# A seven-product group's four sums in one block on VectorE or all on GpSimd, one more group, and a finer copy of the small projection

## The chip, the cores and the metric

One core of one Trainium2 chip runs the whole program. The metric is the device time of one launch in microseconds (us); lower is better. Everything is written out in one kernel file: the instructions of each engine, their order, and the semaphores between the engines.

## The reference

```python
B, T, D, K, U = 2, 4000, 512, 5, 8
h  = gelu(conv1d(x,  w1, K taps))[:, ::2]        # (2, 2000, 512)
f  = gelu(conv1d(h,  w2, K taps))[:, ::2]        # (2, 1000, 512)
fe = f @ w_f                                     # (2, 1000, 512)
ge = g @ w_g                                     # (2, 8, 512)
j  = tanh(fe[:, :, None, :] + ge[:, None, :, :]) # (2, 1000, 8, 512)
out = j @ w_o                                    # (2, 1000, 8, 512)
```

All inputs and the output are bf16. The two convolutions have five taps, padding 2, and keep every second position. The last product is the largest part: 16,000 rows of j by the 512 x 512 matrix w_o.

## The kernel before, in words

**Stages.** Until about 130 us of the profiled execution, TensorE (PE) is mostly busy with the two convolutions. They are cut into 21 units; the first few products of fe and the product ge lie at the end of this stage. From there to about 246 us is the joint stage: the rest of fe, the tanh, and the product with w_o. The 16,000 rows of j are 125 tiles of 128 rows. The 64 activations that make j (`tanh`) each take one row of ge as their bias and up to 1,000 columns of feT as input, and write bf16 into two ring buffers, `jT` and `jX`, from which PE reads.

**Plain tiles and groups of seven.** A tile can be multiplied in the plain way: `Plain` issues four matmuls of 512 columns into one PSUM bank, and the bank is evicted into `ost` and stored. Or four neighbouring tiles form a group (`Seven`): the 2 x 2 block product is done with seven products instead of eight, as Strassen and Winograd do it. A product is four matmuls of 256 columns (two tiles, two blocks of the inner dimension), so a group has 28 of them. For this it needs four sums of blocks of j (`sums`, line 1094, the buffers `ss`), four sums of blocks of w_o (`wsums`, once, the buffer `tw`), and more work behind the products:

- `p1` multiplies into a bank A, and a copy of the result goes to an SBUF buffer `sn` (`keep`).
- `p5` does the same with a bank D.
- `p2` takes a bank of its own, adds the kept product 1 and writes the result to `og` (`out`, an addition on VectorE).
- `p6` accumulates onto bank A, is kept again, and `p3` accumulates onto D and adds that.
- `p7` and `p4` accumulate onto A in turn; each is followed by its own `out`.

Product 6 therefore waits until product 1 has been kept, product 7 until product 6 has been kept, and product 4 until the output of product 7 has been read from the bank. On PE the products of neighbouring groups are interleaved: 1 of this group, 7 of the last, 5, 2, 6, 4 of the last, 3. Fillers stand between them: plain tiles, pieces of the convolution (`piece`) and products of fe. Of the eight banks, `take()` hands out the one that has been free longest.

**FeSeven.** The first quarter of fe is done in the same seven-product way, with sums on VectorE (`fsums`). Its first product needs fT; its `p1` and `p2` take the next banks of the cycle. The bank of product 2 is the one in which ge was computed.

**ge.** `ge` (line 812 and following) does sixteen small matmuls into one bank, 64 columns in all, which ScalarE copies to `geT`.

**Who does which, and in which order.** `Plan` collects all operations of the program in the order in which the program text makes them. The table `ORDER` then lists, for each engine, the numbers of the operations that it issues, as differences from the one before. Operations that may go to one of two engines (`flex`: the evictions and the sums) go where the table has them. `edges` finds from the buffers which operation must wait for which, `schedule` lays the table out in time, and `emit` writes out the instructions with the semaphore waits. So nothing is decided on the chip: every engine issues its list in order, and each instruction waits until the ones it depends on on other engines are done. SyncE (SP) issues nearly all transfers, also from such a list.

In the kernel before, each of the four sums of a group goes to VectorE (DVE) or GpSimd (POOL) by itself. At the end, `emit` adds waits between the two engines by its own timetable: a sum on POOL that would start within 1.5 us behind the start of a sum on DVE waits for that one:

```python
for o in sorted((o for o in ops if o.port), key=lambda o: (self.start[o.idx], o.eng == "pool")):
    if o.eng == "dve":
        near = o.idx
    elif near is not None and self.start[near] > self.start[o.idx] - 1.5:
        o.after.append(near)
```

**The start.** ScalarE (ACT) begins with fourteen activations of one column (`warm`, the loop over `NPRE`), each reading one element of a two-element buffer and writing the other, and each waiting for the one before. Behind them it copies part of the transposed x (`eo`), which the first convolution matmuls read.

Of the kernel before, what the change touches and what calls it, by code (L numbers as in the profile page):

```python
# [30 lines left out]
        4 2 3""",  # L31
    "act": """
# [9 lines left out]
        3 12 7 1 8 1""",  # L42
    "dve": """
# [9 lines left out]
        7 6 17 67 -61 18 -37 46 35 -29 4 17 36 -10 3 -36 13 16 27 7 -21 27 15 -3 9 8 2""",  # L53
    "pool": """
        1 55 1 -55 1 1 1 28 218 1 -217 258 -252 253 8 89 174 150 1 54 -2 1 -31 33 33 2 -1 38 -36 35 40 -38 37 34 2 33
        -32 33 32 -30 31 1 1 33 1 28 1 1 28 155 -154 1 27 2 -1 33 -31 32 1 28 2 -1 31 -29 30 1 26 37 -36 37 1 1 33 34
        -33 34 -32 33 1 29 2 -1 33 2 -1 33 2 -1 35 2 -1 36 2 -1 28 -26 27 1 27 1 27 1 1""",
    "sp": """
        6 15 1 1 1 1 1 1 1 1 1 1 1 2 2 1 1 1 1 2 1 1 1 1 1 248 1 1 1 1 1 1 2 1 1 1 1 1 254 1 1 145 3 33 33 4 1 1 30 4 33
        4 1 1 33 4 31 4 1 1 29 4 29 4 1 1 29 4 25 4 1 1 25 4 25 4 1 1 27 4 27 4 1 1 25 4 25 4 1 1 19 1 11 4 21 11 4 19  # L60
        11 4 17 11 1 1 4 17 11 1 1 4 17 11 4 1 1 19 11 4 21 1 11 4 25 4 23 1 1 4 23 4 19 1 1 7 3 3 5 5""",
}

# [49 lines left out]
class Op:  # L113
    __slots__ = ("eng", "fn", "reads", "writes", "dma", "signal", "count", "sem", "val", "idx", "cost", "pin", "after", "wire", "alt", "port", "slack")


class Plan:
# [12 lines left out]
    def op(self, eng, fn, reads=(), writes=(), cost=0.1):  # L130
        o = Op()
        o.eng, o.fn, o.dma, o.signal, o.idx, o.alt, o.port = eng, fn, False, False, len(self.ops), None, self.port
        o.reads, o.writes, o.cost, o.pin, o.after = tuple(reads), tuple(writes), cost, self.pin, list(self.hold)
        self.ops.append(o)
        return o
# [7 lines left out]
    def dma(self, eng, fn, reads=(), writes=(), sem=None, nbytes=524288, rate=330e3, slack=0.0):  # L143

        o = Op()
        o.eng, o.fn, o.dma, o.signal, o.idx, o.alt, o.port = eng, fn, True, False, len(self.ops), None, False
        o.reads, o.writes, o.cost, o.pin, o.after, o.wire = tuple(reads), tuple(writes), 0.43, True, [], nbytes / rate
        o.slack = slack
        if sem is None:
            sem = [self.nc.alloc_semaphore(f"s_d{o.idx}"), 0]  # L150
        sem[1] += 16
        o.sem, o.val = sem[0], sem[1]
        self.ops.append(o)
        return o
# [81 lines left out]
    def emit(self, block, tail):  # L236
# [3 lines left out]
        near = None  # L240
        for o in sorted((o for o in ops if o.port), key=lambda o: (self.start[o.idx], o.eng == "pool")):
            if o.eng == "dve":
                near = o.idx
            elif near is not None and self.start[near] > self.start[o.idx] - 1.5:
                o.after.append(near)
# [3 lines left out]
        for o in ops:  # L249
            need = {}  # L250
            for j, w in pred[o.idx].items():
                q = ops[j]
# [64 lines left out]
def bass_standalone__seq2seq_rnn_t_joint__speech_kernel(  # L317
# [38 lines left out]
    NPRE = 14  # L356
    TAPS = (0, 4, 2, 1, 3)
    NX = 2

    with ExitStack() as es:  # L360
# [140 lines left out]
        for _ in range(NPRE):  # L501
            act(warm[0:1], warm[1:2], ACT.Gelu_apprx_tanh)
# [311 lines left out]
        def ge():  # L814
            c0 = bank()
            for m in range(NK):
                mm(ps.cols(c0 + m * BU, BU), [(wg_sb[k, m * P:(m + 1) * P], gT[k]) for k in range(NK)], True, True)
            act(geT[:], ps.cols(c0, NK * BU), ACT.Copy)
# [253 lines left out]
        class Seven:  # L1072
# [15 lines left out]
            def sums(self):  # L1088
                S = self.S
                eng = "dve" if self.n in (0, 1) else "pool"  # L1090
                pl.port = True
                for i, x, y, op in ((0, self.a(1, 0), self.a(1, 1), add), (1, S[0], self.a(0, 0), sub),
                                    (2, self.a(0, 0), self.a(1, 0), sub), (3, self.a(0, 1), S[1], sub)):
                    fn = lambda e, o=S[i], x=x, y=y, op=op: e.tensor_tensor(out=o.ap, in0=x.ap, in1=y.ap, op=op)  # L1094
                    alt = {"pool": (fn, 1.12), "dve": (fn, 0.34)}
                    pl.flex({k: alt[k] for k in (("dve", "pool"))}, (x, y), (S[i],))
                pl.port = False
# [130 lines left out]
        gaps = (1, 3, 5, 7)  # L1228
        jts = [2 + 4 * i for i in range(S1)]
        j = 2 + 4 * S1  # L1230
        for n in range(13):
# [75 lines left out]
```

## Time and profile before

| | before |
|---|---|
| time, median of 3 runs | 250.69 us (250.52 to 250.94) |
| the profiled execution: time / span | 250.55 us / 248.7 us |
| PE matmuls, busy | 243.8 us (98%), 1938 on record |
| PE weight loads (PEld), busy | 182.6 us (73%) |
| DVE, busy | 208.0 us (84%) |
| ACT, busy | 197.6 us (79%) |
| POOL, busy | 100.7 us (41%) |
| sums of groups (L1094), in the joint stage | DVE 26, 17.7 us; POOL 86, 98.3 us |
| granted TensorE clock | 1.0 |

The span is what the profile sees, from the first instruction to the last; the time is what the launch took. PEld is the loading of weights into TensorE, which overlaps its matmuls. In the rows below, a line of the timeline has the start in us from the beginning of the span, the length in us, engine, source line, operation, output and inputs, shapes, and how many instructions in a row it stands for; square brackets hold what the engine waited for just before it, and how long. A row of the view of waits has the waiting instruction, an arrow to what released it, and then the sum of the waits, their count, and the longest. A row of windows has the stretch, its length, and the busy time of each engine.

### The profile page before, as it was taken

The numbers are of one execution on the slowest core, as the hardware profiler recorded it, in microseconds if no ns is written. First come the engines' busy times: TensorE is split into PE (matmuls) and PEld (weight loads), VectorE is DVE, ScalarE is ACT, GpSimd is POOL, SyncE is SP. The second block draws the span as 40 slices with busy tenths as digits, with TensorE's granted clock in tenths as the row PEclk, the third lists the DMA queues.
The fourth block names the chain that finished last, engine by engine and source line by source line (L and its number), as shares of the span: only waits on it lengthen the run. The fifth ranks groups of instructions, "written<-read, shape, count | busy, mean of one in ns | idle before, by whom it ended". The sixth has DMA issues, their size and how long they took to land.

```text
span 248.7 us, 5271 instructions
## 1 busy us (share of the span) xinstructions
PE 243.8 (98%) x1938; PEld 182.6 (73%) x1944; DVE 208.0 (84%) x371; ACT 197.6 (79%) x349; POOL 100.7 (41%) x107
## 2 busy tenths in 40 slices
PE   7999999999999999999999999999999999999994
PEld 3879976666666666666566888777788878777883
DVE  1799996967999994796957889778999999996793
ACT  8787948458786475643699999999999999998672
POOL 1000000000000000000008988978799999999530
PEclk9999999999999999999999999999999999999999
DMA  6999999989000061000001043323345554454547
GB/s 212 319 224 179 126 209 173 193 169 355 31 3 0 0 209 48 0 4 0 0 3 42 31 147 106 100 87 127 109 156 161 172 188 162 160 182 137 192 153 249
DMA packets 54871, 31.83 MB, mean 128 GB/s; under 512 B 31902, under 2 KB 54590, under 8 KB 54846
## 3 DMA queue, kind: packets, MB, share of 16 engines
q1 hardware_dynamic: 54558, 31.34, 47.2%
q8 instruction: 15, 0.25, 0.5%
q10 hardware_dynamic: 288, 0.16, 0.2%
q14 instruction: 10, 0.08, 0.1%
HBM read 7.60 MB, written 16.38 MB: 96 GB/s over the span
## 4 chain that ended last, share of the span: by engine, by line
PE 86%; ACT 7%; DMA 2%; issue 1%; DVE 1%; SPq 0%; DVEq 0%; ACTq 0%
PE acc L461 86%; ACT jT L453 3%; DMA w_sb<-in_w_dram 2%; ACT sn L563 1%; ACT og L563 1%; ACT jX L453 1%; DVE og L448 1%; ACT sd L453 1%; DVE sn L564 0%; DVE og L564 0%; PE acc L599 0%; ACT fT L453 0%; SPq L479 0%; SPq L488 0%; ACT ost L453 0%
## 5 line engine op out<-in xcount | busy, mean ns | idle before, releaser
L448 DVE TENSOR_TENSOR og<-acc,sn 128x512 bf16<-128x512 f32 x84 | 54.7, 682 | 5.1 <-PE acc L461 5.1
L453 ACT ACTIVATE jT<-feT,geT 128x1000 bf16<-128x1000 f32 (+5 forms) x60 | 57.5, 1017 | 0.3 <-DVE feT L448 0.3
L1094 POOL TENSOR_TENSOR ss<-jT 128x512 f16<-128x512 bf16 x34 | 39.7, 1182 | 35.2 <-DVE ss L1094 33.3
L461 PE MATMUL acc<-tw,ss 128*128 128x256 f16 x336 | 46.0, 273 | 0.0
L461 PE MATMUL acc<-row,w_sb 128*128 128x334 bf16 (+2 forms) x224 | 39.2, 297 | 0.0
L461 PEld LDWEIGHTS acc<-tw,ss 128*128 128x128 f16 x336 | 32.3, 98 | 7.5 <-ACT sn L563 0.5
L461 PE MATMUL acc<-wo_sb,jT 128*128 128x256 bf16 (+1 forms) x205 | 33.1, 283 | 0.2
L563 ACT ACTIVATE sn<-acc 128x512 f32<-128x512 f32 x48 | 29.7, 628 | 3.4 <-PE acc L461 2.8
L564 DVE COPY sn<-acc 128x512 f32<-128x512 f32 x36 | 24.6, 685 | 6.3 <-PE acc L461 6.0
L453 ACT ACTIVATE hT<-acc 128x334 bf16<-128x334 f32 (+3 forms) x36 | 15.4, 430 | 17.4 <-PE acc L461 16.9
L461 PEld LDWEIGHTS acc<-row,w_sb 128*128 128x128 bf16 x224 | 21.2, 97 | 9.3 <-DVE acc L605 0.7
L453 ACT ACTIVATE sd<-acc 128x334 f32<-128x334 f32 (+2 forms) x48 | 20.5, 432 | 8.7 <-PE acc L461 7.4
L461 PEld LDWEIGHTS acc<-wo_sb,jT 128*128 128x128 bf16 x208 | 20.2, 98 | 5.1
L1094 POOL TENSOR_TENSOR ss<-ss,jT 128x512 f16<-128x512 f16 x19 | 22.3, 1179 | 2.4 <-DVE ss L1094 1.9
L445 POOL MEMSET hT<- 128x8 bf16 (+2 forms) x6 | 0.8, 148 | 55.5 <-ACT hT L453 43.0
L448 DVE TENSOR_TENSOR row<-row 128x1336 bf16<-128x1336 bf16 (+2 forms) x24 | 19.1, 806 | 0.0
L1094 POOL TENSOR_TENSOR ss<-jT,ss 128x512 f16<-128x512 bf16 x15 | 17.5, 1169 | 2.4 <-DVE ss L1094 2.4
L453 ACT ACTIVATE jX<-feT,geT 128x1000 bf16<-128x1000 f32 (+3 forms) x20 | 18.4, 965 | 0.0
L605 DVE SCALAR_TENSOR_TENSOR acc<-acc,sd 128x334 f32<-128x334 f32 (+2 forms) x24 | 11.7, 488 | 7.6 <-PE acc L461 7.5
L461 PE MATMUL acc<-xp,w_t 128*128 128x334 bf16 (+1 forms) x96 | 17.6, 305 | 0.0
L461 PE MATMUL acc<-hT,w_t 128*128 128x334 bf16 x96 | 17.6, 304 | 0.0
L461 PE MATMUL acc<-wo_sb,ss 128*128 128x256 bf16 x112 | 17.1, 273 | 0.0
(129 smaller groups left out, 473.4 us busy)
## 6 DMA issues: line engine op xcount, KB each, us to landing
out_dram<-og SPq DMA_DIRECT2D x42, 256.0 KB, 2.2
w_sb<-in_w_dram SPq DMA_DIRECT2D x10, 512.0 KB, 5.9
out_dram<-og SPq DMA_DIRECT2D x14, 128.0 KB, 2.3
out_dram<-ost SPq DMA_DIRECT2D x10, 128.0 KB, 1.9
xr<-in_x_dram SPq DMA_DIRECT2D x1, 512.0 KB, 3.2
wf_sb<-in_w_f_dram SPq DMA_DIRECT2D x1, 512.0 KB, 4.2
wg_sb<-in_w_g_dram SPq DMA_DIRECT2D x1, 512.0 KB, 5.2
wo_sb<-in_w_o_dram SPq DMA_DIRECT2D x1, 512.0 KB, 6.8
```

The lines of the kernel that those rows point to most:

```text
L445: pl.op("pool", lambda e: e.memset(v.ap, 0.0), (), (v,))
L448: pl.op(eng, lambda e: e.tensor_tensor(out=o.ap, in0=a.ap, in1=b.ap, op=op), (a, b), (o,), 0.02 + 2.14e-3 * o.ap.free_size() if eng == "po ...
L453: pl.op("act", lambda e: e.activation(o.ap, i.ap, func, scale=scale, bias=0.0 if bias is None else bias.ap), rd, (o,), o.ap.free_size() * ...
L461: ins = e.matmul(o.ap, lhsT=l.ap, rhs=r.ap, start=start and n == 0, stop=stop and n == len(pairs) - 1, skip_group_check=not check)
L563: pl.flex({"act": (lambda e: e.activation(o.ap, v.ap, ACT.Copy), 0.05 + n * 0.833e-3), "dve": (lambda e: e.tensor_copy(out=o.ap, in_=v.ap) ...
L564: "dve": (lambda e: e.tensor_copy(out=o.ap, in_=v.ap), 0.065 + n * 1.04e-3)}, (v,), (o,))
L605: pl.op(eng, lambda e: e.scalar_tensor_tensor(out=o.ap, in0=a.ap, scalar=f, in1=b.ap, op0=ALU.mult, op1=add), (a, b), (o,), vec_cost(o, (a ...
L1094: fn = lambda e, o=S[i], x=x, y=y, op=op: e.tensor_tensor(out=o.ap, in0=x.ap, in1=y.ap, op=op)
```

## The change

1. **Sums.** 29 groups of seven instead of 28, and 9 plain tiles instead of 13: the plain tiles that stand between the last groups go from pairs behind groups 1, 3, 5 and 7 of the later list to pairs behind 1 and 5. For ten of the groups (`ONV`, counted from 0) all four sums are on DVE, in one block with nothing of DVE between them: the first one waits for all the inputs of the four, and each of the others stands right behind the one before. For the other nineteen all four are on POOL. The order within a group is now sum 0, 2, 1, 3. The rule in `emit` is gone; in its place is a table, `AFTER`, with ten pairs: one sum on POOL that waits for the last sum of a block on DVE.
2. **geT.** The copy of the 64 columns of ge from PSUM to `geT` is cut in 24 (`NG`) copies of two or three columns, all on ACT.
3. **warm.** One activation instead of fourteen.
4. **The order.** `ORDER` is written anew for all engines. In the convolutions a few of the evictions and of the scaled copies have changed places between ACT and DVE. In the joint stage, products and fillers stand in a partly different order on PE. The engines' lists differ as follows: PE has 16 matmuls of 512 columns less and 28 of 256 more. DVE has 40 sums instead of 26, three more of the additions that write `og`, three more plain copies to `og`, one copy to `ost` less, and one copy to `sn` less. ACT has four copies to `sn` more, two to `og` less, three to `ost` less, 24 copies to `geT` instead of one, and one `warm` instead of fourteen. POOL has 76 sums instead of 86. Of the 24 copies to `geT`, the first 22 stand before an activation that makes part of fT, and two behind it.

```diff
 ORDER = {
     "pe": """
-        48 1 1 1 1 1 1 1 3 2 2 6 1 -5 1 1 1 4 1 1 1 1 2 2 1 1 1 1 1 1 1 1 1 1 1 1 1 1 1 1 1 1 1 1 1 1 1 68 11 15 -24 1
+        35 1 1 1 1 1 1 1 3 2 2 6 1 -5 1 1 1 4 1 1 1 1 2 2 1 1 1 1 1 1 1 1 1 1 1 1 1 1 1 1 1 1 1 1 1 1 1 68 11 15 -24 1
...
+AFTER = """
+    779:726 780:748 817:854 928:963 1091:1060 1120:1244 1213:1153 1317:1346 1408:1445 1566:1538"""
...
-        near = None
-        for o in sorted((o for o in ops if o.port), key=lambda o: (self.start[o.idx], o.eng == "pool")):
-            if o.eng == "dve":
-                near = o.idx
-            elif near is not None and self.start[near] > self.start[o.idx] - 1.5:
-                o.after.append(near)
+        for word in AFTER.split():
+            i, j = map(int, word.split(":"))
+            ops[i].after.append(j)
...
-    NPRE = 14
+    ONV = (0, 1, 4, 7, 10, 13, 16, 19, 22, 25)
...
+    NG = 24
...
-        for _ in range(NPRE):
-            act(warm[0:1], warm[1:2], ACT.Gelu_apprx_tanh)
+        act(warm[0:1], warm[1:2], ACT.Gelu_apprx_tanh)
...
-            act(geT[:], ps.cols(c0, NK * BU), ACT.Copy)
+            cut = [NK * BU * i // NG for i in range(NG + 1)]
+            for i, j in zip(cut, cut[1:]):
+                act(geT[i:j], ps.cols(c0 + i, j - i), ACT.Copy)
...
-                for i, x, y, op in ((0, self.a(1, 0), self.a(1, 1), add), (1, S[0], self.a(0, 0), sub),
-                                    (2, self.a(0, 0), self.a(1, 0), sub), (3, self.a(0, 1), S[1], sub)):
+                for i, x, y, op in ((0, self.a(1, 0), self.a(1, 1), add), (2, self.a(0, 0), self.a(1, 0), sub),
+                                    (1, S[0], self.a(0, 0), sub), (3, self.a(0, 1), S[1], sub)):
                     fn = lambda e, o=S[i], x=x, y=y, op=op: e.tensor_tensor(out=o.ap, in0=x.ap, in1=y.ap, op=op)
-                    alt = {"pool": (fn, 1.12), "dve": (fn, 0.34)}
-                    pl.flex({k: alt[k] for k in (("dve", "pool"))}, (x, y), (S[i],))
+                    if self.n in ONV:
+                        o = pl.op("dve", fn, (x, y) if i else (x, y, self.a(0, 0), self.a(0, 1)), (S[i],) if i else tuple(S[q] for q in range(4)), 0.34)
+                        o.glue = op is not add
+                        if o.glue:
+                            o.after.append(o.idx - 1)
+                    else:
+                        pl.op("pool", fn, (x, y), (S[i],), 1.12)
...
-        gaps = (1, 3, 5, 7)
+        gaps = (1, 5)
...
-        for n in range(13):
+        for n in range(14):
```

More of the change, by code (lines that the diff above doesn't have):

```diff
@@ L17 @@
     "pe": """
[13 rows of a table removed]
-        4 2 3""",
-    "act": """
[9 rows of a table removed]
-        3 12 7 1 8 1""",
-    "dve": """
[9 rows of a table removed]
-        7 6 17 67 -61 18 -37 46 35 -29 4 17 36 -10 3 -36 13 16 27 7 -21 27 15 -3 9 8 2""",
[13 rows of a table added]
+        3 1 2 1 2 1 2 1 6 1 2 1 7 1 2 1 2 1 -11 1 12 1 2 1 2 1 8 1 -4 1 6 3 3 1 4 2 3""",
+    "act": """
[9 rows of a table added]
+        71 -32 -19 23 27 -37 -55 81 -50 65 -12 18 10 -79 82 8 6 10 13 6 10 11 6 6 15 7 1 8 1""",
+    "dve": """
[9 rows of a table added]
+        3 6 2 8 7 8 3 3 3 63 1 1 1 -42 3 -11 24 19 -26 23 6 -15 40 6 -15 29 7 6 10 6 7 6 10 11 -7 13 6 9 -3 9 8 2""",
     "pool": """
-        1 55 1 -55 1 1 1 28 218 1 -217 258 -252 253 8 89 174 150 1 54 -2 1 -31 33 33 2 -1 38 -36 35 40 -38 37 34 2 33
-        -32 33 32 -30 31 1 1 33 1 28 1 1 28 155 -154 1 27 2 -1 33 -31 32 1 28 2 -1 31 -29 30 1 26 37 -36 37 1 1 33 34
-        -33 34 -32 33 1 29 2 -1 33 2 -1 33 2 -1 35 2 -1 36 2 -1 28 -26 27 1 27 1 27 1 1""",
+        1 42 1 -42 1 1 1 15 218 1 -217 258 -252 253 8 89 174 227 -1 2 35 -34 33 2 1 73 1 1 33 -32 33 1 66 -65 66 1 33
+        -32 33 1 1 57 191 -189 1 -2 28 1 1 1 61 31 -29 -1 2 29 1 64 -63 65 34 -33 34 1 56 -55 56 1 35 -34 33 66 -64 63
+        -62 64 31 -30 31 1 58 -57 58 1 26 -25 53 -29 30 -28 29 -28 29""",
     "sp": """
-        6 15 1 1 1 1 1 1 1 1 1 1 1 2 2 1 1 1 1 2 1 1 1 1 1 248 1 1 1 1 1 1 2 1 1 1 1 1 254 1 1 145 3 33 33 4 1 1 30 4 33
-        4 1 1 33 4 31 4 1 1 29 4 29 4 1 1 29 4 25 4 1 1 25 4 25 4 1 1 27 4 27 4 1 1 25 4 25 4 1 1 19 1 11 4 21 11 4 19
-        11 4 17 11 1 1 4 17 11 1 1 4 17 11 4 1 1 19 11 4 21 1 11 4 25 4 23 1 1 4 23 4 19 1 1 7 3 3 5 5""",
-}
+        6 2 1 1 1 1 1 1 1 1 1 1 1 2 2 1 1 1 1 2 1 1 1 1 1 248 1 1 1 1 1 1 2 1 1 1 1 1 254 1 1 168 3 33 33 4 1 1 30 4 33
+        4 1 1 33 4 31 4 1 1 29 4 29 4 1 1 29 4 25 4 1 1 25 4 25 4 1 1 27 4 27 4 1 1 25 4 25 4 1 1 19 1 11 4 21 11 4 25 4
+        25 1 1 4 19 11 4 1 1 17 11 4 27 1 1 4 27 4 25 1 1 4 25 4 23 1 1 4 23 4 19 1 1 7 3 3 5 5""",
+}
+AFTER = """
+    779:726 780:748 817:854 928:963 1091:1060 1120:1244 1213:1153 1317:1346 1408:1445 1566:1538"""
 class View:
@@ L113 @@
 class Op:
-    __slots__ = ("eng", "fn", "reads", "writes", "dma", "signal", "count", "sem", "val", "idx", "cost", "pin", "after", "wire", "alt", "port", "slack")
+    __slots__ = ("eng", "fn", "reads", "writes", "dma", "signal", "count", "sem", "val", "idx", "cost", "pin", "after", "wire", "alt", "port", "slack", "glue")
 class Plan:
@@ L132, in op @@
         o.eng, o.fn, o.dma, o.signal, o.idx, o.alt, o.port = eng, fn, False, False, len(self.ops), None, self.port
+        o.glue = False
         o.reads, o.writes, o.cost, o.pin, o.after = tuple(reads), tuple(writes), cost, self.pin, list(self.hold)
@@ L146, in dma @@
         o.eng, o.fn, o.dma, o.signal, o.idx, o.alt, o.port = eng, fn, True, False, len(self.ops), None, False
+        o.glue = False
         o.reads, o.writes, o.cost, o.pin, o.after, o.wire = tuple(reads), tuple(writes), 0.43, True, [], nbytes / rate
```

60 rows, old and new, of the table ORDER are left out of this document.

## The prediction

> **What bounds the kernel now.** I read the page first, then the view of waits, then the timeline at each place where TensorE (PE) or its weight loads (PEld) waited.
>
> ```profile
> span 248.7 us, 5271 instructions
> PE 243.8 (98%) x1938; PEld 182.6 (73%) x1944; DVE 208.0 (84%) x371; ACT 197.6 (79%) x349; POOL 100.7 (41%) x107
> ```
> ```profile
> POOL ss L1094 <- DVE ss L1094: 39.3, 10, 32.6
> PEld acc L461 <- ACT eo L453: 0.9, 1, 0.9
> PEld acc L461 <- DVE acc L605: 0.7, 3, 0.2
> PEld acc L461 <- ACT sn L563: 0.5, 2, 0.3
> PEld acc L461 <- DMA w_sb<-in_w_dram: 0.3, 1, 0.3
> ```
> ```profile
> 130.00:246.00 116.00, 115.29 (x952) 92.37 (x956) 101.43 (x167) 109.28 (x169) 98.33 (x86) 1.00 0.43 139
> ```
>
> PE is busy 98% of the span, but a busy PE may still be a waiting one, because ends of matmuls are modelled. So the waits count: after the start (the eo and w_sb rows) PE's loads wait only some tenths of a us in all. The second thing to see is which row is missing: no row has PE or PEld waiting for a sum of POOL (GpSimd) or of DVE. The 39.3 us in the first row are POOL's own waiting for DVE, 32.6 of them before the joint stage began. In that stage (the last row: PE, PEld, DVE, ACT, POOL) all four are nearly full, but only PE's matmuls stand end to end. So the time falls by what is taken from PE's list and from its few gaps, and rises by each wait that becomes longer than what PE has queued in front of it. Faster sums alone are worth nothing.
>
> **Part 1: 29 groups instead of 28.** Four plain tiles (16 matmuls, 512 wide) leave; one group (28 matmuls, 256 wide) comes. What a matmul costs is the distance of the starts, not its modelled duration:
>
> ```profile
> 130.87 0.81 PE L461 MATMUL acc<-wo_sb,jT 128*128 128x512 bf16 x3
> 131.52 0.73 PE L461 MATMUL acc<-row,w_sb 128*128 128x334 bf16 x4
> ...
> 239.34 1.04 PE L461 MATMUL acc<-tw,ss 128*128 128x256 f16 x8
> 240.21 0.60 PE L461 MATMUL acc<-wo_sb,jX 128*128 128x256 bf16 x4
> ```
>
> Three starts of 512 in 131.52 - 130.87 = 0.65 us: 0.217 each. Eight of 256 in 0.87: 0.109 each. So 16 x 0.217 - 28 x 0.109 = 3.47 - 3.05 = **0.42 us less PE work**. With PE end to end, all of it is on the path.
>
> **Part 2: the gaps in the joint stage.** There are two, both a keep of product 1 (sn) that ACT does late, so that product 6, which writes the same bank, waits:
>
> ```profile
> 176.95 1.02 ACT L453 ACTIVATE jX<-feT,geT 128x808 bf16<-128x808 f32 x1
> 177.05 1.04 PE L461 MATMUL acc<-tw,ss 128*128 128x256 f16 x8
> 177.81 1.13 ACT L563 ACTIVATE sn<-acc 128x512 f32<-128x512 f32 x2
> 177.93 0.60 PE L461 MATMUL acc<-wo_sb,jT 128*128 128x256 bf16 x4
> 178.51 0.33 PEld L461 LDWEIGHTS acc<-tw,ss 128*128 128x128 f16 x4 [0.26 <-ACT sn L563]
> ```
> ```profile
> 187.14 1.09 ACT L563 ACTIVATE sn<-acc 128x512 f32<-128x512 f32 x2
> 187.29 0.60 PE L461 MATMUL acc<-wo_sb,jT 128*128 128x256 bf16 x4
> 187.80 0.33 PEld L461 LDWEIGHTS acc<-tw,ss 128*128 128x128 f16 x4 [0.19 <-ACT sn L563]
> ```
>
> Four matmuls from 177.93 end their turn at 178.37; the next start is at 178.51: 0.14 us lost, since ACT was inside a tanh when product 1 ended. From 187.29 likewise 187.73 against 187.80: 0.07. These are groups 9 and 12 (counted from 0). In the new order group 9's keep of product 1 is DVE's, with no tanh ahead of it, and around group 12 ACT has the keeps of products 5 and 1 in a row with no tanh between. Both gaps should go: **0.21 us**. What is late next is the ordinary distance from product 1 to product 6, mostly three products of 0.44 us, in which a keep of 0.6 us fits. The three short waits behind DVE acc (L605) I leave where they are.
>
> **Part 3: sums in blocks.** DVE's sums go from 26 to 40, POOL's from 86 to 76.
>
> ```profile
> L1094 POOL TENSOR_TENSOR ss<-jT 128x512 f16<-128x512 bf16 x34 | 39.7, 1182 | 35.2 <-DVE ss L1094 33.3 <-DVE og L448 0.9 <-PE acc L461 0.9
> L1094 DVE TENSOR_TENSOR ss<-jT,ss 128x512 f16<-128x512 bf16 x8 | 6.9, 863 | 0.0
> L448 DVE TENSOR_TENSOR tw<-wo_sb x2: 420/422/425, 115.7 to 116.0; 128x512 f16<-128x512 bf16 x2
> 237.09 4.87 DVE L448 TENSOR_TENSOR og<-acc,sn 128x512 bf16<-128x512 f32 x8
> ```
> ```profile
> 130.00:246.00 116.00, 17.74 (x26) 98.33 (x86) 1.00 0.43 139
> ```
>
> A sum alone on DVE takes 0.42 us (the weight sums tw, least, middle and most in ns, with POOL idle); beside POOL's sums 0.86. A block without POOL is 4 x 0.42 = 1.7 us; if its first sum meets one of POOL's, up to 1.18 more, 2.9. The Trainium skill, page "SBUF — State Buffer", section "SBUF: two separate sides", calls this an exclusive lock of the shared port pair: whichever engine starts first holds it for its instruction. The rows agree (0.86 against 0.42). By that rule too a block pays at most once, and the sum stays as it is.
>
> DVE: 40 x 0.42 = 16.8 us, with ten full collisions 28.6, against 17.7 for the 26 of before (the last row above, that of the joint stage's sums on DVE and POOL; 0.68 each); also four more evictions (three og additions, three og copies, one ost and one sn less), 0.61 each by the row at 237.09 (4.87 / 8): 2.4. That is +1.5 to +13 us, likelier +4, since a collision rarely meets a POOL sum at its very start. DVE idles 116 - 101.4 = 14.6 us in the stage, so it fits, less easily than before. POOL: ten sums less, 11.8 us; its waits for ten blocks, 17 us, replace some 6.7 (39.3 - 32.6): about as full as before, and nobody waited for it. ACT: three ost and two og less, four sn more: one eviction less. The cost to PE I take as **zero**; the cover is what PE has between a product and the next use of its bank. The first eviction behind most blocks has 2.2 to 2.9 us. If that cover fails the price is the second rival's.
>
> **Part 4: the geT copy in 24 pieces.** ACT reads ge's bank in 24 copies of 2 or 3 columns: 22 before an fT activation, two after it. FeSeven's product 2 overwrites that bank, so PE waits for the last copy.
>
> ```profile
> 2.03 3.25 ACT L453 ACTIVATE warm<-warm 128x1 f32<-128x1 f32 x14
> ```
> ```profile
> 115.70 0.22 ACT L453 ACTIVATE geT<-acc 128x64 f32<-128x64 f32 x1
> 116.85 0.45 ACT L453 ACTIVATE fT<-acc 128x334 bf16<-128x334 f32 x1 [0.93 <-PE acc L461]
> 117.79 1.01 PE L461 MATMUL acc<-fT,wf_sb 128*128 128x504 bf16 x4
> 118.64 0.73 PE L461 MATMUL acc<-row,w_sb 128*128 128x334 bf16 x4
> ...
> 130.35 0.46 ACT L453 ACTIVATE sd<-acc 128x334 f32<-128x334 f32 x1
> 130.68 1.15 ACT L453 ACTIVATE jT<-feT,geT 128x1000 bf16<-128x1000 f32 x1
> ...
> 229.08 0.59 ACT L563 ACTIVATE sn<-acc 128x512 f32<-128x512 f32 x1
> 229.56 0.60 ACT L563 ACTIVATE og<-acc 128x512 bf16<-128x512 f32 x1
> ```
>
> PE reaches product 2 at 117.79 + 2 x 0.85/4 = 118.22. From PSUM, 334 columns hold ACT 0.33 us and 512 hold it 0.48, so 0.05 us is left at no column. At that price the 22 copies end at 116.80, before fT could start anyway (116.85); fT, two copies and 0.2 us until the result counts end at 117.5: hidden, 0.7 us to spare. The cover fails when 115.70 + 24c + 0.33 + 0.2 passes 118.22: **c over 0.083 us**. The upper bound is the first row, that of warm, 3.25/14 = 0.23 (each waits there for the one before; the copies don't wait for each other): 121.8, 3.5 us late. I take 0.05, the row of the same kind of source. The Trainium skill, page "ScalarE: Activation LUTs", section "What ACT_TABLE_LOAD costs", speaks against it: 186 ns plus 0.833 ns a column, neighbours overlapping by about 93 ns. By that a copy is an estimated 0.095 us, the last one 0.3 us late, and the sum 250.4. The PSUM rows above (0.05) do not agree with it.
>
> **Part 5: 13 warm activations less.**
>
> ```profile
> 5.18 1.55 ACT L453 ACTIVATE eo<-acc 128x256 bf16<-128x256 bf16 x3
> 5.88 3.90 PE L461 MATMUL acc<-eo,w_sb 128*128 128x254 bf16 x32 [0.69 <-ACT eo L453]
> 7.86 1.64 PEld L461 LDWEIGHTS acc<-eo,w_sb 128*128 128x128 bf16 x16 [0.33 <-DMA w_sb<-in_w_dram]
> ```
>
> ACT's eo copies stood behind the warm ones (from 2.03 for 3.25) until 5.18; they can now start some tenths earlier, and so can PE's first 16 matmuls. But the next 16 wait at 7.86 for a weight transfer, which nothing here moves. The gain ends there: zero.
>
> **The sum.** The profiled execution took 250.55 us (span 248.7, 1.85 around it), 0.14 under the median of 250.69. 250.55 - 0.42 - 0.21 = 249.92; on the median's footing 250.06, taken as **250.1** (-0.24%). 0.2% is 0.50 us, about what a measurement of this kernel can tell from no change; 250.19 is the border.
>
> **Rivals.**
> *The groups alone.* The rewritten order opens as much gap elsewhere as it closes: 250.69 - 0.42 = 250.3, within 0.2%. For it: gaps of 0.1 us are finer than an order laid down in advance can be expected to steer. Against: the two named ones have a cause that is gone. 0.27.
> *The blocks hold evictions back (slower).* Between product 7 of group 7 and its product 4, which needs that bank, stand three products of 0.44 and an fe product of four 501-wide matmuls (0.85, as the 504-wide ones above): 2.2 us. A block that begins 0.9 us before product 7 ends and collides (2.9) frees DVE 2.0 us after; the eviction takes 0.6 and 0.1 to be seen: 0.5 us late. It decides where a block collides in full and the eviction behind it has under 2.7 us; three or four such places of ten give +1.5 to +2: 251.5. For it: DVE's means show collisions are common. Against: PE waits for no DVE eviction in this stage now. 0.15.
> *The small copies cost more than 0.05 (slower).* With c at 0.15, 115.70 + 3.6 + 0.53 = 119.8: 1.6 us late, 251.7; the saving is eaten from c = 0.109, and 0.2% above from 0.13. For it: no row shows so small a copy from PSUM. Against: the straight line through the rows. 0.13.
> *The sums change nothing*: that is part of my forecast; it is worth zero either way.
>
> **Numbers.** Forecast 0.45, faster. Groups alone 0.27, same. The two slower ones 0.15 + 0.13 = 0.28. The range begins at 249.8 (all small DVE waits gone as well, and the scatter of the runs) and ends at 251.3, which leaves out the worse half of the slower cases. The forecast's own range is 249.8 to 250.3.
>
> **What would show it.** PE: 16 fewer 512-wide and 28 more 256-wide matmuls, no row PEld behind ACT sn at groups 9 and 12. FeSeven's product 2 at 118.2 without a wait behind ACT geT, the copies 0.05 apart. DVE sums of 0.42 except the first of a block. Wrong it is if PE waits for DVE og or sn behind a block, for geT, or for a POOL sum.

## The result and the profile after

The changed kernel takes 250.03 us (median of 12 runs, 249.78 to 250.45) against 250.66 us for the kernel before on the same chip: ratio 0.9975, 95% interval 0.9966 to 0.9984. On another chip it was 250.23 against 250.84, 0.9974 (0.9965 to 0.9983). It is faster by a quarter of a per cent, as forecast; 250.1 was predicted.

The page of the changed kernel, its joint stage (windows view; PE, PEld, DVE, ACT, POOL, then the clock), and its waits:

```profile
span 248.3 us, 5299 instructions
PE 244.0 (98%) x1956; PEld 184.5 (74%) x1956; DVE 212.5 (86%) x390; ACT 195.2 (79%) x357; POOL 88.0 (35%) x97
```
```profile
130.00:246.00 116.00, 115.36 (x969) 93.34 (x967) 105.00 (x185) 109.27 (x168) 85.53 (x76) 1.00 0.43 139
```
```profile
POOL ss L1097 <- DVE ss L1097: 13.7, 8, 1.8
...
PEld acc L463 <- ACT sn L564: 1.0, 5, 0.2
...
PEld acc L463 <- DVE acc L606: 0.5, 1, 0.5
```

PE still bounds the kernel. POOL now waits for DVE in eight places, 1.7 us each on average (the ten new waits; where the block is long done, no time is lost). But PE's loads wait longer than before behind ACT's keeps (1.0 us in five places, 0.5 in two before), and there is one new wait behind DVE. So the two gaps that were to close did not make the joint stage shorter. Where the time came from is seen by cutting the span at three matmuls: the first that reads xa, the first of FeSeven, and the row that holds the last twelve. First the changed kernel, then the kernel before (its row of FeSeven, at 117.79, stands in the prediction):

```profile
19.72 1.05 PE L463 MATMUL acc<-xa,w_x 128*128 128x206 bf16 x10
...
117.58 1.01 PE L463 MATMUL acc<-fT,wf_sb 128*128 128x504 bf16 x4
...
244.11 1.26 PE L463 MATMUL acc<-wo_sb,jX 128*128 128x256 bf16 x12
```
```profile
19.62 1.23 PE L461 MATMUL acc<-xa,w_x 128*128 128x206 bf16 x12
...
244.34 1.26 PE L461 MATMUL acc<-wo_sb,jX 128*128 128x256 bf16 x12
```

| stretch, us | before | changed | difference |
|---|---|---|---|
| start to xa | 19.62 | 19.72 | +0.10 |
| convolutions, xa to FeSeven | 98.17 | 97.86 | -0.31 |
| FeSeven to the last row (the joint stretch) | 126.55 | 126.53 | -0.02 |
| last row to the end of the span | 4.36 | 4.19 | -0.17 |
| span | 248.7 | 248.3 | -0.4 |

The first stretch scatters with the landing of the weights (19.3 to 20.1 in the profiles of this study). The others repeat. The convolutions take 97.86 in the changed kernel, in its repeat and in runs 3 and 10, and 98.08 in run 12, which has the old order there. The last two stretches, with the new joint stage and nothing else that touches them, are 126.49 to 126.54 and 4.2 in four profiles; with the old one, 126.55 to 126.57 and 4.36 to 4.45 in three.

The matmuls of the joint stretch are shorter by 0.40 (the sum of the usual start distances), so about as much must be lost in waits. Taken as the distance of two starts less the usual one, the waits after 130 us add up to 0.56 in eight places of over 0.03 us, against 0.26 in three in the kernel before; and 0.15 against 0.06 lie between 112 and 130 us. The kernel's lists tell which product each of the eight belongs to. Five of them, 0.42 together, wait for a keep on ACT that stands behind a tanh: those of product 5 in groups 10, 15 and 19 (product 3 waits) and of product 6 in groups 11 and 19 (product 7 waits). The other three are of 0.04 to 0.05: behind a keep on DVE, an output on DVE and a copy of the last convolution units. One of the five:

```profile
184.61 0.99 ACT L455 ACTIVATE jX<-feT,geT 128x752 bf16<-128x752 f32 x1
185.42 1.64 ACT L564 ACTIVATE sn<-acc 128x512 f32<-128x512 f32 x3
```
```profile
185.60 0.60 PE L463 MATMUL acc<-wo_sb,jT 128*128 128x256 bf16 x4
186.14 1.05 PE L463 MATMUL acc<-tw,ss 128*128 128x256 f16 x8
```

Four starts from 185.60 end at 186.04; the next, product 7 of group 11, is at 186.14, when the first keep, that of its product 6, is out (the keep began at 185.42, as the tanh let go). It is the pattern of 178.5 before, in another group and for another product: there product 6 waited for the keep of product 1. The others of over 0.1 us end at 198.06 and 212.15.

### The profile page after: what moved, and what is told of

Same layout as the page of the kernel before. It is cut to its first block, busy times and chain, and to the rows that moved or that the text cites. A ratio compares the mean times of both kernels' runs of the same rounds, so it can differ in the third digit from the quotient of the medians.

```text
span 248.3 us, 5299 instructions
## 1 busy us (share of the span) xinstructions
PE 244.0 (98%) x1956; PEld 184.5 (74%) x1956; DVE 212.5 (86%) x390; ACT 195.2 (79%) x357; POOL 88.0 (35%) x97
## 4 chain that ended last, share of the span: by engine, by line
PE 96%; DMA 3%; SPq 0%; ACT 0%; issue 0%
PE acc L463 95%; DMA w_sb<-in_w_dram 3%; PE acc L600 0%; SPq L481 0%; SPq L490 0%; ACT ost L455 0%
## 5 line engine op out<-in xcount | busy, mean ns | idle before, releaser
L450 DVE TENSOR_TENSOR og<-acc,sn 128x512 bf16<-128x512 f32 x87 | 56.7, 683 | 4.4 <-PE acc L463 3.7
L455 ACT ACTIVATE jT<-feT,geT 128x1000 bf16<-128x1000 f32 (+5 forms) x60 | 58.3, 1021 | 1.2 <-DVE feT L450 1.2
L463 PE MATMUL acc<-tw,ss 128*128 128x256 f16 x348 | 48.3, 273 | 0.0
L1097 POOL TENSOR_TENSOR ss<-jT 128x512 f16<-128x512 bf16 x28 | 32.3, 1162 | 44.3 <-ACT jT L455 38.3
L463 PEld LDWEIGHTS acc<-tw,ss 128*128 128x128 f16 x348 | 33.7, 98 | 6.5 <-ACT sn L564 0.4
L564 ACT ACTIVATE sn<-acc 128x512 f32<-128x512 f32 x52 | 32.3, 655 | 3.4 <-PE acc L463 3.3
L565 DVE COPY sn<-acc 128x512 f32<-128x512 f32 x35 | 23.7, 685 | 2.4 <-PE acc L463 1.9
L1097 POOL TENSOR_TENSOR ss<-jT,ss 128x512 f16<-128x512 bf16 x16 | 18.5, 1159 | 6.8 <-DVE ss L1097 5.1
L1097 POOL TENSOR_TENSOR ss<-ss,jT 128x512 f16<-128x512 f16 x16 | 18.6, 1162 | 1.8 <-DVE ss L1097 1.7
L463 PE MATMUL acc<-wo_sb,ss 128*128 128x256 bf16 x116 | 17.8, 273 | 0.0
```

The lines of the kernel that those rows point to most:

```text
L450: pl.op(eng, lambda e: e.tensor_tensor(out=o.ap, in0=a.ap, in1=b.ap, op=op), (a, b), (o,), 0.02 + 2.14e-3 * o.ap.free_size() if eng == "po ...
L455: pl.op("act", lambda e: e.activation(o.ap, i.ap, func, scale=scale, bias=0.0 if bias is None else bias.ap), rd, (o,), o.ap.free_size() * ...
L463: ins = e.matmul(o.ap, lhsT=l.ap, rhs=r.ap, start=start and n == 0, stop=stop and n == len(pairs) - 1, skip_group_check=not check)
L564: pl.flex({"act": (lambda e: e.activation(o.ap, v.ap, ACT.Copy), 0.05 + n * 0.833e-3), "dve": (lambda e: e.tensor_copy(out=o.ap, in_=v.ap) ...
L565: "dve": (lambda e: e.tensor_copy(out=o.ap, in_=v.ap), 0.065 + n * 1.04e-3)}, (v,), (o,))
```

## The experiments

Each was run beside the kernel before on its chip. In seven of the fourteen profiles a small transfer of x (xe) lands some 2.5 us later than in the others, and PE waits 0.6 to 1.3 us at about 59 us. The times of the kernel before scatter as widely on the two chips where these seven were taken (250.02 to 252.59). This scatter makes the medians of the first eight runs wide, and what is read from them, but for run 5, rests on the stretches of the table.

**1 and 2. The convolution's order.** The first takes the part of ORDER ahead of ge from the changed kernel into the kernel before; the second does the reverse.

```diff
 ORDER = { ... }   # only the entries of operations ahead of ge, for all engines
```

> The kernel before, with the convolution stage's part of the order tables (all that is issued ahead of ge's product, its few evictions and scaled copies that change places between ACT and DVE too) taken from the changed kernel; groups, sums, geT and warm as before. The prediction has no term for this part: by it the time stays at 250.66 us, within 0.1. Rival: in the two traces five waits of PE in that stage (at 22.7, 27.5, 30.3, 31.1 and 78.1 us, 0.25 us in all) are gone in the changed kernel; if the new order closed them, the time falls by some 0.25 to 0.3, to 250.4, and these waits are missing here too.

Measured: 250.66 against 250.83, 0.9993 (0.9972 to 1.0014).

> The changed kernel with the convolution stage's part of the order tables as it was before. By the prediction's sum nothing of the gain is lost: 250.0 us. By the rival the five waits of 0.25 us come back: 250.3, and what is left of the gain (0.3 to 0.4) is the 29th group's 0.40 less the waits that the new order opens in the joint stage.

Measured: 250.94, 1.0003 (0.9980 to 1.0026). Both undecided by their times; both profiles have the late transfer. What can be compared is the time from the first xa matmul to the 300th behind it (about 55 us), ahead of that place: 35.33 in the kernel before (35.24 in run 12, which has the same order there), 35.11 with the new order alone (run 1), 35.12 with the old order and one warm (run 2), 35.10 with the new order and fourteen warm (run 4), 35.06 in the changed kernel and its repeats. So the new order takes most of the waits there away, and so, in the one profile that there is, does taking thirteen warm activations from ACT's start; the two do not add up. Behind 60 us the wait at 78 us (0.04) is gone in run 1 and in the changed kernel. In run 2 it is 0.50, behind the late transfer. That the convolutions give 0.2 to 0.3 us is shown by the stretches (97.86 against 98.08 and 98.17); how much of it is the order's and how much the warm ones' is not settled.

**3 and 10. geT in one copy.**

```diff
-    NG = 24
+    NG = 1
...   # ORDER and AFTER: the same lists, renumbered for 23 operations fewer
```

> The changed kernel with geT copied at once instead of in 24 pieces. The prediction has the pieces hidden: 250.0 us, no change. Rival from the trace after: the pieces start 0.053 us apart but end 0.065 apart, the fT activation behind them ends 0.3 us later, the sum sf on DVE waits for it (0.36), the addition onto PSUM behind that (L606) is late and PE waits 0.15 at 118.4. By that this kernel is 0.15 us faster, 249.9, and PE has no wait at that place.

Measured: 250.01 against 250.83, 0.9971 (0.9951 to 0.9991).

> geT in one copy, once more, on the same chip as the changed kernel. By its trace (no wait of PE at 118.4, the same waits after it) 0.15 us below the changed kernel: 249.9. If the pieces cost nothing: 250.0.

Measured: 250.04 against 250.84, 0.9967 (0.9955 to 0.9980), beside 250.23 for the changed kernel: 0.19 us less, with intervals that overlap. The timeline of the changed kernel, then that of run 10, shows where it goes:

```profile
115.49 1.55 ACT L455 ACTIVATE geT<-acc 128x3 f32<-128x3 f32 x22
116.66 0.72 ACT L455 ACTIVATE fT<-acc 128x334 bf16<-128x334 f32 x1
...
117.41 0.68 DVE L450 TENSOR_TENSOR sf<-fT 128x1008 bf16<-128x1008 bf16 x1 [0.36 <-ACT fT L455]
...
118.01 0.51 DVE L606 SCALAR_TENSOR_TENSOR acc<-acc,sd 128x334 f32<-128x334 f32 x1
118.57 0.40 PEld L463 LDWEIGHTS acc<-row,w_sb 128*128 128x128 bf16 x4 [0.47 <-DVE acc L606]
```
```profile
115.65 0.22 ACT L456 ACTIVATE geT<-acc 128x64 f32<-128x64 f32 x1
...
116.81 0.45 ACT L456 ACTIVATE fT<-acc 128x334 bf16<-128x334 f32 x1 [0.93 <-PE acc L464]
...
117.74 1.01 PE L464 MATMUL acc<-fT,wf_sb 128*128 128x504 bf16 x4
...
244.12 1.26 PE L464 MATMUL acc<-wo_sb,jX 128*128 128x256 bf16 x12
```

Twenty-two pieces start within 116.66 - 115.49 = 1.17 us, 0.053 each. But fT behind them takes 0.72 instead of 0.45: the pieces' ends lie 0.065 apart, and the backlog is handed on. DVE waits for fT, its next sums and the addition onto PSUM are late, and PE, whose four matmuls from 117.58 end their turn at 118.43, starts again only 0.15 later. With one copy the joint stretch is 126.38 (244.12 - 117.74; run 3 has the same to 0.02), 0.15 less. The pieces cost 0.15 us.

**4. Fourteen warm activations.**

```diff
-        act(warm[0:1], warm[1:2], ACT.Gelu_apprx_tanh)
+        for _ in range(14):
+            act(warm[0:1], warm[1:2], ACT.Gelu_apprx_tanh)
```

> The changed kernel with fourteen warm activations again. By the prediction (the second half of the first tap waits for its weights, from 7.9 us on, whatever ACT does ahead of it): no change, 250.0 us, PE's first eo matmul about 0.16 us later. Rival: the earlier eo copies are worth those 0.16 us, and this kernel takes 250.2.

Measured: 250.53 against 250.83, 0.9981 (0.9959 to 1.0003): undecided, with the late transfer in its profile. PE's first eo matmul starts at 5.88 and the second set of 16 at 7.78; in the profiles with one warm activation they start at 5.7 to 6.0 and 7.6 to 8.1. The stretch from the start to xa is not longer (19.54), and the next 300 matmuls take 35.10 instead of 35.06.

**5. Without POOL's ten waits.**

```diff
-    779:726 780:748 817:854 928:963 1091:1060 1120:1244 1213:1153 1317:1346 1408:1445 1566:1538"""
+    """
```

> The changed kernel without the ten waits that make a sum on POOL stand back for a block on DVE (the AFTER table is empty; nothing else changes). Then POOL's sums run into the blocks. By the prediction's prices a block that is hit once takes 1.7 + 1.18 = 2.9 us instead of 1.7, and its sums take more than the 0.455 us on average that they take now (0.55 to 0.9). Forecast's side (PE's cover is enough): PE's waits stay as in the changed kernel, time 250.0 us. Rival (blocks hold evictions back): three or four blocks cost PE some 0.5 us each, time 251.5, with new waits of PE behind og or sn of DVE.

Measured: 260.43 against 250.93, 1.0388 (1.0343 to 1.0433). That is some ten us above the changed kernel, where the rival had 1.5. In the profile the joint stretch is 136.02, 9.5 more than 126.53, and the late transfer adds 1.2 ahead of it. One block, DVE, then POOL and PE in the same stretch; and the same block of group 25 in the changed kernel:

```profile
231.13 2.65 DVE L1097 TENSOR_TENSOR ss<-jT 128x512 f16<-128x512 bf16 x2
233.70 1.37 DVE L1097 TENSOR_TENSOR ss<-ss,jT 128x512 f16<-128x512 f16 x1
235.11 1.26 DVE L1097 TENSOR_TENSOR ss<-jT,ss 128x512 f16<-128x512 bf16 x1
236.28 0.68 DVE L565 COPY sn<-acc 128x512 f32<-128x512 f32 x1
```
```profile
231.05 1.15 POOL L1097 TENSOR_TENSOR ss<-jT 128x512 f16<-128x512 bf16 x1
232.16 1.33 POOL L1097 TENSOR_TENSOR ss<-jT,ss 128x512 f16<-128x512 bf16 x1
233.46 1.33 POOL L1097 TENSOR_TENSOR ss<-jT 128x512 f16<-128x512 bf16 x1
234.75 1.33 POOL L1097 TENSOR_TENSOR ss<-ss,jT 128x512 f16<-128x512 f16 x1
```
```profile
233.57 0.60 PE L463 MATMUL acc<-wo_sb,jT 128*128 128x256 bf16 x4
237.02 0.61 PE L463 MATMUL acc<-tw,ss 128*128 128x256 f16 x4 [2.85 <-DVE sn L565]
```
```profile
223.55 0.88 DVE L1097 TENSOR_TENSOR ss<-jT 128x512 f16<-128x512 bf16 x2
224.34 0.42 DVE L1097 TENSOR_TENSOR ss<-ss,jT 128x512 f16<-128x512 f16 x1
224.80 0.42 DVE L1097 TENSOR_TENSOR ss<-jT,ss 128x512 f16<-128x512 bf16 x1
```

DVE and POOL take turns: each of the block's four sums waits for the sum of POOL that began ahead of it, 1.26 to 1.37 us instead of 0.42. The block takes 5.2 us instead of 1.7, the keep behind it starts at 236.28, and PE stands still for 3.0 us. Six of the ten blocks are hit in two to four of their sums; four meet POOL hardly or not at all. PE's long waits (0.62, 2.21, 1.17, 0.94 and 3.01 us) add up to 7.9 of the 9.5. Most of the rest is the clock. After the wait of 2.2 us at 177.4 it is lower (windows view, PE, then the granted clock):

```profile
176.00:180.00 4.00, 1.96 (x15) 1.00 0.15 45
180.00:184.00 4.00, 4.00 (x24) 0.57 0.22 70
184.00:188.00 4.00, 4.00 (x39) 1.00 0.39 133
```

From 180.3 to 183.7, 3.4 us, the starts of 256-wide matmuls lie 0.213 apart, not 0.109: 3.4 x (1 - 0.109/0.213) = 1.7 us lost. The Trainium skill, page "TensorE: Matmul & The Clock Gate", section "Part 1: The HAM clock gate (the "warmup" mystery)", has the clock halved after an idle window of about 3.4 us and full again after as long a busy one. The 3.4 us agree; here 2.2 us without a matmul were enough, while the 3.0 us at 234.0 did not lower it.

**6 and 7. The price of a group against four plain tiles.** Run 6 issues 28 matmuls of 256 columns twice, run 7 16 of 512.

```diff
-                for n, (l, r) in enumerate(pairs):
+                for n, (l, r) in list(enumerate(pairs)) * reps:   # reps = 2 for the chosen ones
...
```

> The changed kernel with 28 matmuls of 256 columns issued twice (products 1, 5 and 2 of groups 14 to 17 and two of group 18, the first of their two tiles; the second issue writes the same values again). This is the PE work of one more group, with nothing for the other engines. If PE stands end to end and a start costs 0.109: 28 x 0.109 = 3.05 us more, 253.1. Rival: part of it falls into PE's waits (0.2 us of them lie in those groups), so 2.8 to 2.9 more.

Measured: 254.91 against 250.93, 1.0147 (1.0110 to 1.0183).

> The changed kernel with 16 matmuls of 512 columns issued twice (four of the nine plain tiles; the second issue writes the same values again). By 0.2165 us a start: 16 x 0.2165 = 3.46 us more, 253.5, and 0.4 us more than the run with 28 more of 256: that difference is the price of four plain tiles against one group. Rival: a start of either width costs something beside its columns that hides here, and the two come out the same.

Measured: 254.41, 1.0127 (1.0099 to 1.0156). The medians do not tell them apart, and their order is even the wrong way round, with intervals that overlap: both profiles have the late transfer, and in that of run 6 the last transfer ends 6.0 us behind the last row instead of 4.2. The joint stretch does. Run 6, then run 7:

```profile
117.94 1.01 PE L466 MATMUL acc<-fT,wf_sb 128*128 128x504 bf16 x4
...
247.23 1.26 PE L466 MATMUL acc<-wo_sb,jX 128*128 128x256 bf16 x12
```
```profile
118.53 1.01 PE L466 MATMUL acc<-fT,wf_sb 128*128 128x504 bf16 x4
...
248.44 1.26 PE L466 MATMUL acc<-wo_sb,jX 128*128 128x256 bf16 x12
```

129.29 - 126.53 = 2.76, and 129.91 - 126.53 = 3.38. In run 6 the waits at 198 and 212 us are gone (0.28 instead of 0.56): 2.76 + 0.28 = 3.04, that is 0.109 for each of 28. In run 7 0.10 of them are gone (0.46): 3.48, 0.217 for each of 16. The difference is 0.44, near the 0.42 of the prediction; without the waits put back it is 0.62. And what PE gets on top fills its waits first, as the rival of run 6 said.

**8 and 11. The keeps ahead of the tanhs.** On top of one copy of geT, three evictions go from ACT to DVE, and seven neighbours in the two lists change places.

```diff
-    NG = 24
+    NG = 1
...
 ORDER = {  # joint stage: group 4's and 9's og of product 4, group 19's keep of product 6
-    "act": ... (these three among others)
+    "dve": ... (these three among others)
```

> The changed kernel with geT copied at once and with three evictions of the joint stage moved from ACT to DVE (group 4's and group 9's output of product 4, group 19's keep of product 6) and a few neighbours on the two lists changed in place, so that the keeps that PE waits for stand ahead of a tanh or are DVE's. In the changed kernel PE loses 0.148 us behind geT's pieces and some 0.55 in eight waits of the joint stage, most of them behind such a keep on ACT. Theory: these are what eats the gain of the two old gaps; without them the time is 0.4 to 0.6 lower than the changed kernel's, 249.4 to 249.6. Rival: new waits open as the old ones close, 249.9, as without geT's pieces alone.

Measured: 250.21 against 250.93, 0.9973 (0.9951 to 0.9996), with the late transfer in its profile. The joint stretch is 126.07. The waits for keeps behind a tanh are gone, but there is one of 0.22 at 195.5 behind an output on DVE, whose buffer a store still held.

> geT in one copy and three evictions on DVE, once more, on the same chip as the changed kernel. By its first trace (0.11 us of waits in the joint stage instead of 0.55, none behind geT) 0.45 to 0.6 us below the changed kernel: 249.4 to 249.6. Rival: other waits outside that stage take it back, 249.9.

Measured: 249.68 (249.29 to 249.87) against 250.84, 0.9954 (0.9942 to 0.9967), and 0.55 us below the changed kernel beside it. The kernel is that of run 8.

```profile
117.29 1.01 PE L464 MATMUL acc<-fT,wf_sb 128*128 128x504 bf16 x4
...
243.18 1.26 PE L464 MATMUL acc<-wo_sb,jX 128*128 128x256 bf16 x12
```

The joint stretch is 125.89, 0.65 less than in run 9; the waits after 130 us are 0.12, and that of run 8 at 195.5 is not among them. So the late keeps and the pieces of geT were what ate the gain, and this version is the fastest of the study.

**9. The changed kernel again,** without any edit.

> The changed kernel itself once more, as the measure for the two beside it. 250.0 us, ratio to the kernel before 0.9975; between FeSeven's first product and the last matmul 127.5 to 127.6 us, as in its first profile and in the runs that change only what lies ahead of it.

Measured: 250.23 against 250.84, 0.9974 (0.9965 to 0.9983). Its joint stretch is 126.54, with the same eight waits.

**12. The kernel before without its rule.**

```diff
-        near = None
-        for o in sorted(...):
-            ...
-                o.after.append(near)
```

> The kernel before without its own rule that makes a sum on POOL stand back for one on DVE that starts within 1.5 us ahead of it; nothing else changes. Theory: it was these waits, then as now, that kept POOL from holding DVE up, and without them DVE's 26 sums, 0.69 us on average with the rule, take 0.9 or more, PE waits behind evictions of DVE, and the time rises by several us, 253 or more, as it did by 10 in the changed kernel. Rival: single sums are hit once each and their evictions have cover enough, so that only blocks of four need the waits: 250.7, no change.

Measured: 250.98 against 250.84, 1.0000 (0.9990 to 1.0010). The sums of that run on DVE and POOL:

```profile
130.00:246.00 116.00, 20.43 (x26) 99.37 (x86) 1.00 0.43 139
```

20.4 us instead of 17.7 on DVE, and PE waits after 130 us about as before (0.28, against 0.26). The theory was wrong and its rival right: in the kernel before, where the sums stand singly between evictions, the 2.7 us that they lose on DVE have cover, and the waits on POOL are worth nothing. The blocks of the changed kernel need theirs (run 5).

## Why the prediction was right, and where it was not

The time and the sign were right; the sum behind them was partly not. It had -0.42 for matmuls and -0.21 for two gaps. The profiles show about -0.40 for matmuls, +0.38 for waits from FeSeven on, -0.31 in the convolutions (-0.22 against run 12) and -0.17 behind the last row. The last two have no term in the prediction, and make up for its second. That the total met the forecast is therefore luck: the matmuls' term held, but new waits took it back, and the gain came from places that the sum does not name.

- **Part 1** holds: 0.40 us for the 29th group by the usual start distances, 0.44 by runs 6 and 7.
- **Part 2** failed. The two named gaps did go, for the reason given. But "what is late next" was read from the distance of products 1 and 6 alone, and no wait of the new order is of that kind: most are for keeps of products 5 and 6 that queue behind a tanh on ACT, and 0.26 became 0.56. One of them, at 186.14, stands at the head of the very row of keeps on ACT that the prediction named for group 12. This is the mechanism of the rival "the groups alone"; that its 250.3 was not measured is owed to the convolutions and the tail. Run 11 shows what the forecast's step would have been worth: with its waits down to 0.12 and without geT's pieces, the joint stretch is 0.66 below the 126.55 of the kernel before, where Parts 1 and 2 had 0.63 together.
- **Part 3** had the outcome right, zero, and one step wrong. DVE's 40 sums take 17.4 us (16.8 to 28.6 forecast), because POOL stands back. But "a block pays at most once" is wrong: run 5 has it paying up to four times, since POOL's next sum gets its turn between two of the block's. The rival's price for held-up evictions, 1.5 to 2 us, was five times too small, and the condition that decides it is the table of ten waits, which the prediction had entered only as lost time of POOL. The Trainium skill, page "SBUF — State Buffer", section "SBUF: two separate sides", gives the lock for one instruction; the rows agree, and taking it for a block was the prediction's own error.
- **Part 4**: 0.053 us a piece, 0.05 taken; the last copy is out at 117.51, and product 2 of FeSeven does not wait. The estimate by the Trainium skill's page "ScalarE: Activation LUTs", section "What ACT_TABLE_LOAD costs", 0.095, does not hold for these copies from PSUM. The step that failed is the cover: only PE's wait for the bank was counted, not who waits for the fT activation behind the pieces. That cost 0.15 (runs 3 and 10).
- **Part 5**: PE's second set waits for its weights, as said: it starts at 7.6 to 8.1 us with one warm activation and at 7.8 to 7.9 with fourteen. Behind xa the new order shows 0.04 us of difference (run 4); in the old one it may be more (run 2).
- **The convolutions and the tail.** The order was said to be rewritten there, and five waits of 0.25 us in all could be found in the trace of before, but only the three behind L605 were looked at and left where they are. Why the last transfers end 0.17 us earlier was not tried. Of the 0.6 us between the medians, the stretches explain 0.4 to 0.5; the rest lies within the interval and stays open.

## What to carry to other kernels

When an engine is near the limit, count what a rewritten order closes and opens over the whole span, stage by stage; gaps of 0.1 us that one names by hand are replaced by others unless the order is made against the queue in front of the late step. A copy cut in pieces must be followed to the consumer of the instruction behind it, not only to the next writer of its bank. And a block of sums on VectorE is only a block if GpSimd is made to wait for its end: the wait that looks like lost time is what the block lives on.

## What the runs showed of the hardware

- A copy of 2 or 3 columns from PSUM on ACT starts every 0.053 us but ends every 0.065; over 24 of them the length of one grows from 0.17 to 0.47 us, and the activation behind them is 0.27 us longer.
- POOL and DVE sums take turns: 1.26 to 1.43 us for a DVE sum between two of POOL (0.42 alone), 1.33 for a POOL sum (1.16 alone).
- The granted clock of PE fell to half for 3.4 us after one wait of 2.2 us, from 0.7 us after work had begun again, and not after another of 3.0.
- One small transfer of x makes part of the scatter between runs of one kernel: in seven of fourteen profiles PE waits 0.6 to 1.3 us for what hangs on it at about 59 us. Runs 8 and 11 are one kernel; of the 1.65 us between their spans, 0.75 are this wait, 0.77 the start up to xa, and 0.19 the joint stretch. In this row of run 5 POOL waits for the transfer; the row of the kernel before has 18.3:

```profile
POOL xp L545 <- DMA xe<-in_x_dram: 20.5, 1, 20.5
```
